# Three places in a hand-ordered mixer: a join after the activation sums, a forward set one channel pair earlier, token output's sums ahead of a forward set

## The chip, the cores and the metric

The kernel runs on one core of one Trainium2 chip. The metric is the device time of one execution in microseconds (us); lower is better. All data are float32. The abbreviations of the profile are used: PE is TensorE's matrix multiplication and PEld its weight load, DVE is VectorE, ACT is ScalarE, POOL is GpSimd and SP is the queue that issues most transfers.

## The reference

Eight sequences of 3008 tokens with 256 channels pass a global filter and then an MLP mixer.

```python
# x (8, 3008, 256), filt_r and filt_i (1505, 256)
X = np.fft.rfft(x, axis=1)
y = np.fft.irfft(X * (filt_r + 1j * filt_i), n=3008, axis=1)      # the filter
# w_tok1 (3008, 256), w_tok2 (256, 3008), w_ch1 (256, 1536), w_ch2 (1536, 256)
h = np.maximum(y.transpose(0, 2, 1) @ w_tok1, 0.0) @ w_tok2      # token mixing
u = y + h.transpose(0, 2, 1)
out = u + np.maximum(u @ w_ch1, 0.0) @ w_ch2                     # channel mixing
```

## The kernel before

**The mixer's items.** The program is one list of instructions for each engine, in an order that is written out by hand: each engine works off its own list and waits where a value or a buffer is not ready. The main loop, `mix`, goes over 288 items: 8 sequences b, 6 blocks of tokens m (512 wide, the last 448), and 6 channel pairs jp. An item works out two of the twelve 128-channel tiles of the hidden layer for one block. Both products of the channel mixing are done with seven half-size products in place of eight, which costs sums on DVE.

One item i issues, in this order:

- `up_first` (PE, L844): four products of u and of its sums v into the two PSUM tiles `ps_pg` (the two banks of that name, which every item uses); ACT copies one of them (L847).
- `up_middle` (DVE): the sum that the text calls u2, and a double sum s, both read `ps_pg`.
- one waiting step of `todo_v` (a list of small DVE steps), then `h_sums` (DVE) on item i-1's activated `hh`, which makes its four tiles t, and the first half of `down` (PE, L878) for item i-1. This is **place 0**.
- `up_last` (PE, L860): three more products into `ps_pg`; two DVE additions that leave the hidden values in `hh` (in the text: the hidden additions), each with its ReLU on ACT (L865); one more waiting step. This is **place 1**.
- the second half of `down` for item i-1 (four products with t). Where item i-1 was the last pair of its block, six steps of `finish` go into `todo_v`, and the first two, `a` and `b_`, are done at once: they read the four output banks `ps_po`, which the next item's `down` starts to fill anew. This is **place 2**.

All these DVE additions go through the helper `v` and stand in the profile as L822.

**The token mixing** for the next sequence lies inside this loop. At the third pair of a sequence's last block (item 32 of its 36) `token_sums` puts 48 products into one of the two PSUM banks `ps_acc` and `ps_b` (L721). At pairs 4 and 5 of that block `u_part` (L765) makes block 0 of the next u; `v_steps` then leaves two DVE steps in `todo_v`: the first makes two of the v tiles from u, the second (`t24`, two additions of 128x256) makes the other two. The next item, the first of the next sequence, reads all v in its `up_first`.

**The filter** of later sequences is another list of steps, `dft`, a generator which the main loop resumes at given places. Sequences are filtered in groups: (1, 2) beside the mixer of sequence 0; (3, 4) beside that of 1 and 2; (5, 6) beside 3 and 4; (7) beside 5 and 6. Each group ends with 16 pairs of frequencies, and a pair has three steps:

- "b", `b_pair`: the forward set, four small products (L501) into both `ps_acc` and `ps_b`, two DVE multiplications with the filter (L644) that read a bank each, and the issue of the loads for the pair two further on (SP);
- "m", `join`: two DVE operations on these products (L649, L650);
- "i", `bi_pair`: the inverse set, again four small products into the two banks, two ACT copies out of them (L630), and two stores (SP).

For the last three groups a table says at which (jp, place) the step that comes next is run, so a block of six items holds two frequency pairs:

```python
due = (jp, place) in {"b": ((5, 1), (2, 1)), "m": ((0, 0), (3, 0)), "i": ((1, 0), (3, 2))}[coming]
```

A generator step goes behind what its place names and ahead of what comes next. So the forward set at (5, 1) is joined at (0, 0) of the next block, between `h_sums` and `up_last`'s additions on DVE, and its inverse set follows at (1, 0). In the sequences 1, 3 and 5 these steps run on through the last block; in 2, 4 and 6 they are done before it, and in 7 there are none. The group (3, 4) or (5, 6) has twice the width of the group (7) in each of these operations.

Of the kernel before, what the change touches and what calls it, by code (L numbers as in the profile page):

```python
# [41 lines left out]
JP = JT // 2  # L42
# [3 lines left out]
MT = 6  # L46
# [73 lines left out]
def kernel(  # L120
# [591 lines left out]
    def t4_load(b, c, lo=PARTS[0], hi=P, queue=nc.sync):  # L712
        if lo == 0:
            t4[b, c] = t4p.tile([P, TC4, D], FP32, tag="t4", name="t4")
        queue.dma_start(t4[b, c][lo:hi], rows_of(g_d, b)[lo:hi, ts(c, TC4), :])
# [66 lines left out]
    def w2m_load(m):  # L782
        hw = width(m) // 2
        nc.sync.dma_start(w2m[m % 2][:, :, 0:hw], w2_d[m, :, :, 0:hw])
# [148 lines left out]
    def u_part(b, m, i):  # L933
        if i == 0:
            uts[b, m] = up.tile([P, DH, 512], FP32, tag="u", name="u")
        (u_quarter if b else u_unit)(b, m, h1s[b], uts[b, m], i)
# [13 lines left out]
    def one_step():  # L950
        if todo_v:
            todo_v.pop(0)()

    def mix(next_ready):

        wait = []
        pos, hhs, tts = {}, {}, {}

        def loads(b):
            if b + 1 < B and next_ready(b):  # L960
                for c in wait:
                    t4_load(b + 1, c)
                wait.clear()


        own = ({(4, 2): (0, 1)}, {(3, 0): (0,), (4, 0): (1,), (4, 2): (2, 3)})
        new = {(JP - 2, 0): (0, 1), (JP - 1, 0): (2, 3)}

        def u_parts(b, m, jp, place):
            parts = own[b > 0] if m + 1 < MT else new if b + 1 < B else {}  # L970
            now = parts.get((jp, place), ())
            b, m = (b, m + 1) if m + 1 < MT else (b + 1, 0)
            for part in now:
                u_part(b, m, part)
            if now and now[-1] == max(p for ps in parts.values() for p in ps):
                if m:
                    wait.append(m)
                todo_v.extend(v_steps(b, m))
                if b and (b, m) < (B - 1, MT - 2):
                    w2m_load((m + 2) % MT)  # L980

        to_dram = [f for m in range(MT) for f in w2_sums(m)]
        items = [(b, m, jp) for b in range(B) for m in range(MT) for jp in range(JP)]
        n = MT * JP
        for i in range(len(items) + 1):
            now, old = i < len(items), i >= 1
            if ended[0] < len(tiles):
                convert()
            if now:
                b, m, jp = items[i]  # L990
                if i % n == 0:
                    wait.append(0)
                w = width(m)
                hhs[i] = hp.tile([P, 4, 256], FP32, tag="hh", name="hh")
                g = [bank("pg").rearrange("p (s n) -> p s n", s=2) for _ in range(2)]
                s = up_first(jp, uts[b, m], vts[b, m], w, g)
                up_middle(hhs[i], w, g, s)
            one_step()
            if old:
                bo, mo, jo = items[i - 1]  # L1000
                tts[i - 1] = tp.tile([P, 4, 256], FP32, tag="t", name="t")
                for f in h_sums(hhs[i - 1], tts[i - 1], width(mo)):
                    f()
                down(mo, jo, 0, hhs[i - 1], tts[i - 1], pos.setdefault((bo, mo), []))
            if now:
                u_parts(b, m, jp, 0)
            yield b, i % n, 0
            if ended[0] < len(tiles):
                convert()
            if now:  # L1010
                up_last(jp, uts[b, m], vts[b, m], w, g, s, hhs[i])
            one_step()
            loads(b)
            yield b, i % n, 1
            if old:
                down(mo, jo, 1, hhs.pop(i - 1), tts.pop(i - 1), pos[bo, mo])
                if jo == JP - 1:
                    todo_v.extend(finish(bo, mo, uts[bo, mo], pos[bo, mo]))
                    one_step()
                    one_step()  # L1020
            if now:
                if b + 1 < B and i % n == n - 4:
                    h1s[b + 1] = token_relu(b + 1, token_sums(b + 1))
                u_parts(b, m, jp, 2)
                if jp == JP - 1:
                    while todo_v and m + 1 == MT:
                        one_step()
                if i >= 8 and to_dram:
                    to_dram.pop(0)()
                if i in (28, 29):  # L1030
                    w2m_load(i - 28)
            loads(b)
            yield b, i % n, 2
        while todo_v:
            one_step()

    with tc.manual_schedule():
        nc.sync.dma_start(wa0, wa0_d)
        nc.vector.memset(turned[:, A:K2, :], 0.0)
        for t in filts:  # L1040
            nc.vector.memset(t, 0.0)
        half = 0
        second = dft(GROUPS[1])
        for i, _ in enumerate(dft(GROUPS[0])):
            if i == 0:
                nc.scalar.dma_start(wai_t, wait_d)
            k = i - NXC - 2

            if i < NXC:
                if i in (1, 3, 5, 7, 9):  # L1050
                    start()
                if i == NXC - 1:
                    copies()
                    for t, src in ((wa, wa_d), (was, was_d), (wai, wai_d), (ident, ident_d)):
                        nc.scalar.dma_start(t, src)
            elif k >= 0:
                if k == K2 - 5:
                    pause.append(True)
                while half < 2 * IN_B * (k + 1) // K2:
                    if half % 2:  # L1060
                        convert_end()
                    else:
                        convert_middle()
                    half += 1

                if 19 <= k < 25:
                    t4_load(0, k - 19, 0, PARTS[1])
                elif 26 <= k < 29:
                    for c in range(2):
                        t4_load(0, 2 * (k - 26) + c, PARTS[1], PARTS[2])  # L1070
                elif k in (30, 31):
                    for c in range(3):
                        t4_load(0, 3 * (k - 30) + c, PARTS[2], PARTS[3])
        pause.clear()

        fill(5)
        for c in range(A // TC4):
            t4_load(0, c, PARTS[3], P, (nc.sync, nc.gpsimd)[c % 2])
        both = wcp.tile([P, 2, JP, 7, P], FP32, tag="wc", name="wc")

        chan.extend((both[:, 0], both[:, 1]))
        next(second)
        for i in range(IN_B, A // 2 + TC * W2G):
            convert()
            if i == A // 2 + BY_PE - 1:
                sum_up()
                acc = token_sums(0)

        ahead[0](XF, nc.gpsimd)
        h1s[0] = token_relu(0, acc)  # L1090
        for dh in range(DH):
            convert()
            u_part(0, 0, dh)
        for f in v_steps(0, 0):
            f()
        for _ in range(XB):
            next(second)
        group, todo, done = -1, iter(()), True

        def next_ready(b):  # L1100
            return done or b != GROUPS[group][-1]

        coming = "a"
        for b, i, place in mix(next_ready):
            if group + 1 < len(GROUPS) and b == GROUPS[group + 1][0]:
                if not done:
                    raise AssertionError("the filter's steps don't fit beside the mixer's")
                group += 1  # L1110
                done = group + 1 == len(GROUPS)
                todo = iter(()) if done else dft(GROUPS[group + 1]) if group else second
                coming = "a"
            if done:
                continue
            jp = i % JP
            if coming in "aw":
                due = place == 1 or group == 0
            elif group:
                due = (jp, place) in {"b": ((5, 1), (2, 1)), "m": ((0, 0), (3, 0)), "i": ((1, 0), (3, 2))}[coming]  # L1120
            else:
                due = (jp - (coming == "i")) % JP in ((5, 1, 2, 3) if i < 4 * JP else (5, 0, 1, 2, 3)) and place == {"b": 1, "m": 2, "i": 0}[coming]
            if due:
                coming = next(todo, "end")
                done = coming == "end"
# [30 lines left out]
```

## Time and profile before

| | |
|---|---|
| time, median of 3 runs | 2497.85 us (2496.29 to 2501.91) |
| profiled execution, its time | 2499.35 us |
| profiled execution, its span of instructions | 2497.6 us |
| mean granted TensorE clock | 0.993 |
| busy in the span: PE, PEld, DVE, ACT, POOL | 97%, 79%, 74%, 27%, 24% |
| PE busy from 300 to 2300 us | 98.5% to 99.7% in each stretch of the seven looked at |

The time of the profiled execution is 1.75 us more than its span. Shares are of the span from the first to the last instruction. A row of a timeline gives the start, the length, the engine, the line, the operation with what it writes and reads, how many instructions are merged, and in brackets the idle time of the engine ahead of it with what ended it. A row of the waits gives the total in us, how often, and the longest one. A 128x256 product stands as two matmul records.

### The profile page before, as it was taken

The numbers are of one execution on the slowest core, as the hardware profiler recorded it, in microseconds if no ns is written. First come the engines' busy times: TensorE is split into PE (matmuls) and PEld (weight loads), VectorE is DVE, ScalarE is ACT, GpSimd is POOL, SyncE is SP. The second block draws the span as 40 slices with busy tenths as digits, with TensorE's granted clock in tenths as the row PEclk, the third lists the DMA queues.
The fourth block names the chain that finished last, engine by engine and source line by source line (L and its number), as shares of the span: only waits on it lengthen the run. The fifth ranks groups of instructions, "written<-read, shape, count | busy, mean of one in ns | idle before, by whom it ended". The sixth has DMA issues, their size and how long they took to land.

```text
span 2497.6 us, 33945 instructions
## 1 busy us (share of the span) xinstructions
PE 2420.1 (97%) x11836; PEld 1962.4 (79%) x11836; DVE 1846.7 (74%) x3404; ACT 678.6 (27%) x1348; POOL 598.4 (24%) x1086
## 2 busy tenths in 40 slices
PE   7888999999999999999999999999999999999997
PEld 3556676877788777887778877897888888898887
DVE  7686878587885878667885788758786678757776
ACT  5633222133221222223221222213221222212221
POOL 6473332212111211211121112111212112212121
PEclk9999999999999999999999999999999999999999
DMA  9973444254321222335332323314322121301100
GB/s 217 252 206 118 123 131 144 76 170 131 109 82 53 82 82 61 94 99 172 89 94 62 86 71 83 103 45 126 86 77 72 49 70 43 98 24 29 39 16 18
DMA packets 173122, 236.07 MB, mean 95 GB/s; under 512 B 33213, under 2 KB 123067, under 8 KB 172952
## 3 DMA queue, kind: packets, MB, share of 16 engines
q1 hardware_dynamic: 128344, 175.53, 24.1%
q0 software_dynamic: 33376, 48.46, 7.8%
q10 hardware_dynamic: 11232, 9.92, 1.3%
q8 instruction: 94, 1.54, 0.3%
q14 instruction: 76, 0.62, 0.1%
HBM read 156.56 MB, written 77.22 MB: 94 GB/s over the span
## 4 chain that ended last, share of the span: by engine, by line
PE 44%; DVE 5%; issue 1%; DMA 0%; ACT 0%; DVEq 0%; POOL 0%; SPq 0%; ACTq 0%; POOLq 0%
PE ps_po L878 17%; PE ps_pg L844 10%; PE ps_pg L860 7%; PE ps_b L721 2%; PE ps_acc L721 2%; PE ps_b L765 2%; PE ps_acc L765 2%; DVE t L822 1%; DVE hh L822 1%; PE ps_acc L501 1%; DVE p L644 1%; PE ps_b L501 1%; PE ps_b L743 1%; PE ps_acc L743 1%; DVE s L822 1%
## 5 line engine op out<-in xcount | busy, mean ns | idle before, releaser
L925 POOL DMA_DIRECT2D out_dram<-r x757 | 412.5, 553 | 1672.4 <-ACT hh L865 1408.4
L822 DVE TENSOR_TENSOR hh<-ps_pg,s 128x512 f32<-128x512 f32 (+3 forms) x864 | 482.6, 586 | 390.2 <-ACT s L847 386.8
L865 ACT ACTIVATE hh<-hh 128x512 f32<-128x512 f32 (+1 forms) x576 | 348.3, 623 | 986.2 <-DVE hh L822 986.2
L878 PE MATMUL ps_po<-t,wc 128*128 128x256 f32 (+1 forms) x2304 | 546.6, 380 | 4.2 <-DVE t L822 3.1
L878 PEld LDWEIGHTS ps_po<-t,wc 128*128 128x128 f32 x2304 | 426.3, 190 | 132.4 <-DVE t L822 41.1
L844 PE MATMUL ps_pg<-v,wc 128*128 128x256 f32 (+1 forms) x1728 | 415.5, 377 | 2.1 <-DVE v L822 2.1
L878 PE MATMUL ps_po<-hh,wc 128*128 128x256 f32 (+1 forms) x1728 | 413.5, 375 | 0.2 <-ACT hh L865 0.2
L844 PEld LDWEIGHTS ps_pg<-v,wc 128*128 128x128 f32 x1728 | 327.8, 191 | 43.5 <-DVE v L822 5.9
L878 PEld LDWEIGHTS ps_po<-hh,wc 128*128 128x128 f32 x1728 | 329.1, 191 | 38.2 <-ACT hh L865 0.5
L860 PE MATMUL ps_pg<-u,wc 128*128 128x256 f32 (+1 forms) x1152 | 295.8, 379 | 6.0 <-DVE hh L822 6.0
L860 PEld LDWEIGHTS ps_pg<-u,wc 128*128 128x128 f32 x1152 | 215.5, 190 | 63.7 <-DVE hh L822 30.5
L822 DVE TENSOR_TENSOR t<-t,hh 128x256 f32<-128x256 f32 (+1 forms) x576 | 245.2, 426 | 19.9
L822 DVE TENSOR_TENSOR s<-ps_pg,hh 128x512 f32<-128x512 f32 (+1 forms) x288 | 196.1, 681 | 30.3 <-DVE hh L822 0.5
L822 DVE TENSOR_TENSOR t<-hh 128x512 f32<-128x512 f32 (+1 forms) x288 | 192.9, 670 | 0.6 <-ACT hh L865 0.6
L847 ACT COPY s<-ps_pg 128x256 f32<-128x256 f32 (+1 forms) x288 | 106.2, 369 | 318.4 <-PE ps_pg L844 316.9
L844 PE MATMUL ps_pg<-u,wc 128*128 128x256 f32 (+1 forms) x576 | 173.8, 383 | 14.0 <-DVE hh L822 14.0
L860 PE MATMUL ps_pg<-v,wc 128*128 128x256 f32 (+1 forms) x576 | 168.8, 375 | 0.0
L844 PEld LDWEIGHTS ps_pg<-u,wc 128*128 128x128 f32 x576 | 105.6, 190 | 51.6 <-DVE hh L822 37.0
L860 PEld LDWEIGHTS ps_pg<-v,wc 128*128 128x128 f32 x576 | 109.3, 190 | 12.6
L822 DVE TENSOR_TENSOR u<-ps_b,u 128x256 f32<-128x256 f32 (+2 forms) x102 | 58.3, 572 | 67.5 <-PE ps_b L765 61.8
L822 DVE TENSOR_TENSOR u<-ps_acc,u 128x512 f32<-128x512 f32 (+2 forms) x108 | 62.4, 577 | 56.5 <-PE ps_acc L765 52.2
L721 PE MATMUL ps_b<-t,w 128*128 128x256 f32 x384 | 83.9, 380 | 8.1 <-DVE p L644 4.7
(140 smaller groups left out, 2464.7 us busy)
## 6 DMA issues: line engine op xcount, KB each, us to landing
w<-w_tmp SPq DMA_DIRECT2D x35, 896.0 KB
out_dram<-r POOLq DMA_DIRECT2D x698, 32.0 KB, 2.7
t<-g_tmp SPq DMA_DIRECT2D x42, 512.0 KB
g_tmp<-t SPq DMA_DIRECT2D x96, 192.0 KB
t<-z_tmp SPq DMA_DIRECT2D x180, 96.0 KB
z_tmp<-t SPq DMA_DIRECT2D x60, 256.0 KB
filt<-in_x_dram SPq DMA_DIRECT2D x90, 128.0 KB
wb<-wbi_t SPq DMA_DIRECT2D x64, 128.0 KB
```

The lines of the kernel that those rows point to most:

```text
L501: nc.tensor.matmul(outs(i, j), stat(i, j), mov(i, j), start=True, stop=True)
L644: nc.vector.tensor_tensor(out=prods[c, h], in0=pss[h].unsqueeze(1).to_broadcast([P, 2, nb, D]), in1=filts[c % FB][:, :, 0, :].unsqueeze(2) ...
L721: nc.tensor.matmul(acc[:, t, :], w1[:, a, ts(t, P)], t4[b, a // TC4][:, a % TC4, :], start=(a == 0 and t == 0), stop=(a == A - 1 and t == ...
L743: nc.tensor.matmul(ps[:, ds(q * P, n)], t4[b, c][:, r, ts(dh, P)], wai[:, 0:n], start=(first and q == 0), stop=(not first and q == 3))
L765: nc.tensor.matmul(ps[:, ds(j * hw, hw)], h1[:, n, :], w2m[m % 2][:, at, 0:hw], start=(i < 2 and j == 0), stop=(j == len(todo) - 1))
L822: nc.vector.tensor_tensor(out=out, in0=in0, in1=in1, op=op)
L844: nc.tensor.matmul(ps[:, 0:hw], chan[0][:, jp, n, :], mov, start=True, stop=True)
L847: nc.scalar.copy(out=s[:, 0], in_=g[0][:, 0, 0:hw])
L860: nc.tensor.matmul(ps[:, 0:hw], chan[0][:, jp, n, :], mov, start=True, stop=True)
L865: nc.scalar.activation(out=hs, in_=hs, func=AF.Relu)
L878: nc.tensor.matmul(po[i][:, j, 0:hw], chan[1][:, jp, n, :], mov, start=(jp == 0 and first == 1), stop=(jp == JP - 1 and last == 1))
L925: q.dma_start(bass.AP(tensor=ob.tensor, offset=ob.offset + row * D + g * cw, ap=[[N1 * D, 32], [D if h else -D, n], [1, cw]]), blocks[ts(g ...
```

## The change

Four lines are altered. After place 1's own waiting step, the last item of every sequence does one more step of `todo_v`; that step is `t24`. In the table, the forward set that was at (2, 1) is run at (1, 1) where the block is the sequence's last, and the join that was at (0, 0) is run at (0, 1). `n` is the number of items of a sequence, 36.

```diff
             one_step()
+            if now and i % n == n - 1:
+                one_step()
             loads(b)
             yield b, i % n, 1
...
         coming = "a"
+        n = MT * JP
         for b, i, place in mix(next_ready):
...
-                due = (jp, place) in {"b": ((5, 1), (2, 1)), "m": ((0, 0), (3, 0)), "i": ((1, 0), (3, 2))}[coming]
+                due = (jp, place) in {"b": ((5, 1), (1 if i >= n - JP else 2, 1)), "m": ((0, 1), (3, 0)), "i": ((1, 0), (3, 2))}[coming]
```

No operation is added or taken away. Sequence 0 takes another line for its due places, which is not changed, and none of its steps come after item 31.

## The prediction

> **What bounds the kernel.** The page's first part comes first: TensorE is busy for nearly the whole span, and everything else is far below it.
>
> ```profile
> PE 2420.1 (97%) x11836; PEld 1962.4 (79%) x11836; DVE 1846.7 (74%) x3404; ACT 678.6 (27%) x1348; POOL 598.4 (24%) x1086
> ```
>
> So only what makes PE stand still can be won or lost. The change touches sequences 1 to 6, hence the waits of PE in two windows: 600 to 1780 us (groups of two sequences) and 1780 to 2250 us (the group of one).
>
> ```profile
> PE ps_pg L844 <- DVE hh L822: 4.7, 16, 0.6
> PE ps_b L721 <- DVE p L644: 3.6, 2, 1.8
> PE ps_pg L844 <- DVE v L822: 1.8, 2, 0.9
> PE ps_po L878 <- DVE t L822: 1.2, 4, 0.4
> ...
> PE ps_b L721 <- DVE p L644: 1.1, 1, 1.1
> PE ps_po L878 <- DVE t L822: 0.8, 2, 0.4
> PE ps_pg L844 <- DVE v L822: 0.3, 1, 0.3
> ```
>
> Every wait of PE there is for DVE. The first row counts 16, as many as there are joins at (0, 0) in these two groups (8 each), and in the timeline each stands behind such a join. One of them, at sequence 2, block 3:
>
> ```profile
> 943.54 1.89 PE L878 MATMUL ps_po<-t,wc 128*128 128x256 f32 x8
> 943.72 0.69 DVE L649 TENSOR_TENSOR p<-p,p 128x512 f32<-128x512 f32 x1
> 944.32 0.69 DVE L650 TENSOR_TENSOR p<-p,p 128x512 f32<-128x512 f32 x1
> 944.92 1.28 DVE L822 TENSOR_TENSOR hh<-ps_pg,s 128x512 f32<-128x512 f32 x2
> 945.64 0.63 ACT L865 ACTIVATE hh<-hh 128x512 f32<-128x512 f32 x1 [4.92 <-DVE hh L822]
> 945.66 0.30 PEld L844 LDWEIGHTS ps_pg<-u,wc 128*128 128x128 f32 x2 [0.63 <-DVE hh L822]
> 945.66 0.70 PE L844 MATMUL ps_pg<-u,wc 128*128 128x256 f32 x2 [0.23 <-DVE hh L822]
> ```
>
> The join holds DVE from 943.72 to 944.92; only then do the hidden additions empty `ps_pg`, which the next item's `up_first` is to fill. Eight matmuls in 1.89 us with 0.38 us each start 0.216 us apart, so a bar reaches 0.16 us into the next: a stall costs PE the idle time shown and 0.16 us more, here 0.40.
>
> The last two places, the token sums (754.50, for a bank) and the first item of sequence 2 (800.04, for v):
>
> ```profile
> 753.24 1.21 DVE L644 TENSOR_TENSOR p<-ps_b,filt 128x1024 f32<-128x1024 f32 x1
> 754.50 0.70 PE L721 MATMUL ps_b<-t,w 128*128 128x256 f32 x2 [1.79 <-DVE p L644]
> ...
> 798.44 1.22 DVE L644 TENSOR_TENSOR p<-ps_acc,filt 128x1024 f32<-128x1024 f32 x1
> 799.57 0.88 DVE L822 TENSOR_TENSOR v<-v,u 128x256 f32<-128x256 f32 x2
> 800.04 1.13 PE L844 MATMUL ps_pg<-v,wc 128*128 128x256 f32 x4 [0.91 <-DVE v L822]
> ```
>
> **What the Trainium skill says.** "Perfetto Trace Analysis", section Identifying the Most-Contended Engine, holds busy matmul time for a bad measure of headroom, since matmuls overlap; section Optimization Strategy has one look for the gaps and what ends them. The trace agrees: the 0.16 us are such an overlap. The same page, section Per-engine timelines, lets a DVE instruction signal only once its writes are acknowledged, the end of its bar. Here the first hidden addition ends at 945.60 (944.92 and 0.68) and PE starts at 945.66: 0.06 us for a hand-over. "VectorE: DVE Perf Modes", section The TRN2 errata, gives (N + 151)/0.96 ns for a float32 two-tensor add: 691 ns for 512 elements, 1224 for 1024. The trace has 0.68 to 0.71 and 1.21 us. I use the trace's.
>
> **Part 1, the join behind the hidden additions (24 joins).** In the 16 wide ones two operations, 1.20 us from start to start, go behind 1.28 us of additions. `up_last` is through at 943.70 (its last row 943.11 and 0.59), `h_sums` at 943.81: the additions can start where the join did, and end near 945.0. `up_first` then follows `down` without a gap. DVE does the same work in the same order of sums, so `a`, the first step of `finish`, stays at 946.12 and the wait for `ps_po` doesn't grow. DVE even gains: its second step there waited 0.36 us for an ACT copy (L890) that stood behind the ReLUs, and these come 1.2 us earlier. So what follows on DVE moves forward by some 0.4 us together with PE. The join is needed at (1, 0), from 948.88; it ends at 946.2.
> Twelve of the 16 stand alone: 4.7 less 0.31 (two, part 2) and 0.67 (two, part 3) is 3.7, and 12 x 0.16 is 1.9: 5.6 us. The two largest (0.57 and 0.65 shown) exceed what DVE can follow; I take off 0.4. **Gain 5.2 us**, between 0 (DVE holds PE up one item later instead) and 5.6. The 8 narrow joins (0.42 us an operation) show no wait of PE: nothing, as both orders are hidden behind `down`; 0.3 us either way.
>
> **Part 2, t24 ahead of the last forward set (ends of sequences 1, 3, 5).** Two additions, 0.88 us, go ahead of two multiplications, 2.4 us. Shown: 0.91, 0.90 and 0.27, with 0.16 each 2.6 us. Where no set lies between (sequences 0, 2, 4, 6) the same place still loses 0.15 us; that stays. Gain 2.1. The multiplications end 0.9 us later, near 800.5, and u2 behind them started at 801.23 after 0.79 us of idle waiting for ACT: it can start at 800.5, so nothing is late. Two of these items have a join stall of part 1 too (0.15 and 0.16 shown), 0.6 us, which goes as well. **Gain 2.7 us**, 1.5 to 3. In the four other sequences no DVE operation lies between the two places: nothing.
>
> **Part 3, the forward set one channel pair ahead of the token sums (3 sets).** It moves all it issues: four products (1.02 us of PE, 0.7 narrow), two multiplications (2.4 us of DVE, 1.3 narrow), 13 issues on SP. SP: the loads are for the pair two further on, over 40 us away; they go ahead of nothing due before that. PE: the set needs the banks that the inverse set of (1, 0) left; ACT's copies out of them end at 744.04, by then 0.5 us earlier, and the set's turn is at 743.6: just in time, at most 0.2 us a set.
> What goes, with 0.16 each: at the token sums 1.79, 1.79 and 1.15 (5.2 us); one item before, waits of `down` for t of 0.17, 0.17 and 0.33 (1.2 us), covered by the set's own products now; the join stall of these blocks, 2 x 0.5 us. Together 7.4 us.
> What comes: at jp 2 the multiplications stand ahead of u2, s, a transpose (0.70), `h_sums`. Counted through on DVE: the multiplications run from 746.45 to 748.85, u2 to 749.24 (`up_last` needs it, and was due at 748.98), s to 749.97, transpose to 750.6, the first of `h_sums` to 751.1. `down` starts at 751.2, the token sums 1.5 us behind it at 752.7 in place of 754.50: 1.8 us twice. The narrow one in the same way: 1920.1 in place of 1921.65, 1.55. **Gain 5.1 us**; a new wait of about 0.8 us for each wide set at jp 2 is what is late next. Bounds 1.5 (the new wait takes the old one's place) and 7.4.
>
> **Sum.** 5.2 + 2.7 + 5.1 = 13.0 us. The profiled execution's span is 2497.6, its time 2499.35: they would be 2484.6 and 2486.3. The median, 2497.85, lies 1.5 us below that execution; from it, **2484.8 us**. A measurement of this kernel can tell about 0.2%, 5.0 us, from no change.
>
> **Rivals.**
> *DVE stays the bound.* It is busy without a gap from the forward set at (5, 1) to jp 1. If it doesn't give up the 0.36 us, the stall of part 1 comes back at jp 1 as a wait for t. For: without a filter step, `down` at pair 1 of the last block already waits 0.44 us for t. Against: the wide joins' next item has none. Then part 1 gives 0, parts 2 and 3 some 5: 2493. Chance 0.14.
> *The early forward set only shifts the wait*, to u2 and t at jp 2, and keeps the banks' copies in PE's way. Part 3 then gives 1.5: 2488.5. Chance 0.14.
> *Slower: the join delays `finish`.* If the hidden additions can't start before the join would have been over anyway, `a` slips by the join's 1.29 us. The next `down` fills `ps_po` at 947.50, and `a`'s first step left it at 946.80: slack of 0.7. With 0.6 us lost 16 times, the old stalls kept (0.4 each), and narrow joins losing 0.4, part 1 costs 13 us against 8 gained: 2503. It decides when `up_last` ends more than 0.7 us behind `h_sums`; here it ends 0.1 before. Chance 0.04.
> The likeliest case keeps 0.68.
>
> **How the numbers follow.** All that is shown gone, and nothing in its place, is 5.6 + 2.7 + 7.4 + 0.3 = 16.0 us: 2481.9; with 2 us for the median, 2480. At the other end the range takes in the first rival: 2493.5. The likeliest case and the second rival are faster by over 0.2%; the first rival lies on the bound, and I give it mostly to no change. Faster 0.84, within 0.2% 0.12, slower 0.04.
>
> **What would show it.** Right: PE's waits at L844 for hh gone (16 to 0 or a few) in 600 to 1780 us; L649 behind the hidden additions; the L890 wait of DVE smaller than 17.7 us; the token sums' wait gone, with a wait of under 1 us for t or u2 before them; the wait for v gone. Wrong: more and longer waits at L878 for t (first rival), waits there of about 1 us in the token sums' items (second), waits at L878 for `ps_po` after each join (third).

## The result, and the profile after

The changed kernel takes 2481.34 us (median of 4 runs, 2479.32 to 2483.14) against 2497.39 us (4 runs, 2496.29 to 2501.91): a ratio of 0.9934 with a 95% interval of 0.9922 to 0.9947. That is faster by 0.66%, some 16 us, where 13.0 us were forecast. The profiled execution took 2483.14 us with a span of 2481.4, which is 16.2 us shorter than the span before.

The busy line of the page hardly moves: the same work is done, with less standing still.

```profile
PE 2417.7 (97%) x11836; PEld 1965.7 (79%) x11836; DVE 1845.1 (74%) x3404; ACT 679.7 (27%) x1348; POOL 598.4 (24%) x1086
```

The waits of PE in the two windows of before, 600 to 1780 us and 1780 to 2250 us (total, times, longest; the three dots part the windows):

```profile
PE ps_po L878 <- DVE t L822: 1.7, 4, 0.4
PE ps_po L878 <- DVE u L822: 0.2, 1, 0.2
...
PE ps_po L878 <- DVE t L822: 0.4, 1, 0.4
```

The 16 waits for the hidden additions (L844 for hh), the three of the token sums (L721) and the three for v are gone. What is new is small: a wait of `down` for `finish`'s first sum (u), and, within the row for t, a wait at pair 2 of the two blocks with a wide early set (0.42 us each), where two smaller ones at pair 1 (0.17 each) have gone.

The timeline at sequence 2, block 3, the join that the prediction showed:

```profile
938.60 1.89 PE L878 MATMUL ps_po<-t,wc 128*128 128x256 f32 x8
938.77 1.28 DVE L822 TENSOR_TENSOR hh<-ps_pg,s 128x512 f32<-128x512 f32 x2
939.49 1.23 ACT L865 ACTIVATE hh<-hh 128x512 f32<-128x512 f32 x2 [3.71 <-DVE hh L822]
939.97 0.68 DVE L649 TENSOR_TENSOR p<-p,p 128x512 f32<-128x512 f32 x1
940.11 0.41 PEld L844 LDWEIGHTS ps_pg<-u,wc 128*128 128x128 f32 x2
940.33 0.59 PE L844 MATMUL ps_pg<-u,wc 128*128 128x256 f32 x2
...
940.62 0.36 ACT L890 COPY r<-ps_po 128x256 f32<-128x256 f32 x1
...
941.17 0.69 DVE L822 TENSOR_TENSOR u<-ps_po,u 128x512 f32<-128x512 f32 x1
...
941.77 0.42 DVE L822 TENSOR_TENSOR r<-ps_po,r 128x256 f32<-128x256 f32 x1
```

The hidden additions start 0.17 us behind `down`'s first matmul, where they started 1.38 us behind it. `up_first` (940.33) follows the eight matmuls of `down` in step: 8 x 0.216 behind 938.60. ACT's copy L890 is done at 940.98, before DVE asks for it at 941.77, so the bracket of 0.36 us that this row had is gone as well. In before, the first two sums of `finish` stood like this:

```profile
946.12 0.68 DVE L822 TENSOR_TENSOR u<-ps_po,u 128x512 f32<-128x512 f32 x1
...
947.17 0.42 DVE L822 TENSOR_TENSOR r<-ps_po,r 128x256 f32<-128x256 f32 x1 [0.36 <-ACT r L890]
```

The second sum started 1.05 us behind the first; now it is 0.60.

The token sums of sequence 1's end, and the first item of sequence 2:

```profile
746.75 1.22 DVE L644 TENSOR_TENSOR p<-ps_b,filt 128x1024 f32<-128x1024 f32 x1
...
750.17 1.78 PE L878 MATMUL ps_po<-t,wc 128*128 128x224 f32 x8 [0.42 <-DVE t L822]
...
751.79 3.40 PE L721 MATMUL ps_b<-t,w 128*128 128x256 f32 x15
```

```profile
794.60 0.88 DVE L822 TENSOR_TENSOR v<-v,u 128x256 f32<-128x256 f32 x2
795.46 1.23 DVE L644 TENSOR_TENSOR p<-ps_b,filt 128x1024 f32<-128x1024 f32 x1
...
796.15 1.46 PE L844 MATMUL ps_pg<-v,wc 128*128 128x256 f32 x6
```

The multiplications end at 747.97, long before the token sums, which start without a bracket; in their place `down`, just ahead of them, waits 0.42 us for t. In the second view the v sums stand ahead of the multiplications, and `up_first` runs through.

**A measure finer than the median.** ACT's copy L847 comes once in every item, so the same items can be compared between two timelines. From the copy of sequence 1's first item to that of sequence 7's last, before takes 501.61 to 2477.17, 1975.56 us; after takes 1959.16. This leaves out the start, where that first copy comes anywhere between 496.2 and 503.6 us in the nine profiles of this study. Inside the stretch the granted clock is 1.00 in all nine, and sequence 7 has no filter step and takes 234.15 to 234.18 us in before, after and the first four experiments, so hundredths count. The gain in this stretch, item by item:

| step | forecast | measured |
|---|---|---|
| 12 wide joins that stand alone | 5.2 | 5.5 (0.45 each) |
| 7 narrow joins that stand alone | 0 | 1.8 (0.21 to 0.32 each) |
| t24, with the join behind it in two places | 2.7 | 3.0 (1.22, 1.22, 0.53) |
| forward set, with the join of its block | 5.1 | 6.2 (2.10, 2.10, 1.97) |
| sum (of unrounded figures) | 13.0 | 16.4 |

### The profile page after: what moved, and what is told of

It is laid out like the page before. It is cut to its first block, busy times and chain, and to the rows that moved or that the text cites. A ratio compares the mean times of both kernels' runs of the same rounds, so it can differ in the third digit from the quotient of the medians.

```text
span 2481.4 us, 33945 instructions
## 1 busy us (share of the span) xinstructions
PE 2417.7 (97%) x11836; PEld 1965.7 (79%) x11836; DVE 1845.1 (74%) x3404; ACT 679.7 (27%) x1348; POOL 598.4 (24%) x1086
## 4 chain that ended last, share of the span: by engine, by line
PE 48%; DVE 2%; DMA 0%; issue 0%; ACT 0%; POOL 0%; SPq 0%; DVEq 0%; POOLq 0%; ACTq 0%
PE ps_po L878 19%; PE ps_pg L844 11%; PE ps_pg L860 8%; PE ps_acc L721 2%; PE ps_b L721 2%; PE ps_b L765 2%; PE ps_acc L765 2%; PE ps_b L501 1%; PE ps_acc L501 1%; PE ps_acc L743 1%; PE ps_b L743 1%; DVE t L822 1%; DVE hh L822 0%; DVE u L822 0%; DVE s L822 0%
## 5 line engine op out<-in xcount | busy, mean ns | idle before, releaser
L844 PE MATMUL ps_pg<-v,wc 128*128 128x256 f32 (+1 forms) x1728 | 415.8, 377 | 0.1
L844 PEld LDWEIGHTS ps_pg<-v,wc 128*128 128x128 f32 x1728 | 328.5, 191 | 40.9 <-DVE v L822 2.6
L860 PE MATMUL ps_pg<-u,wc 128*128 128x256 f32 (+1 forms) x1152 | 295.2, 379 | 5.7 <-DVE hh L822 5.7
L860 PEld LDWEIGHTS ps_pg<-u,wc 128*128 128x128 f32 x1152 | 214.9, 190 | 62.6 <-DVE hh L822 31.4
L847 ACT COPY s<-ps_pg 128x256 f32<-128x256 f32 (+1 forms) x288 | 106.0, 368 | 333.7 <-PE ps_pg L844 332.4
L844 PE MATMUL ps_pg<-u,wc 128*128 128x256 f32 (+1 forms) x576 | 172.4, 381 | 9.3 <-DVE hh L822 9.3
L860 PE MATMUL ps_pg<-v,wc 128*128 128x256 f32 (+1 forms) x576 | 168.7, 375 | 0.0
L844 PEld LDWEIGHTS ps_pg<-u,wc 128*128 128x128 f32 x576 | 107.2, 190 | 41.5 <-DVE hh L822 26.0
L860 PEld LDWEIGHTS ps_pg<-v,wc 128*128 128x128 f32 x576 | 109.2, 190 | 12.6
L721 PE MATMUL ps_acc<-t,w 128*128 128x256 f32 x384 | 83.5, 379 | 0.0
```

The source lines that it names most:

```text
L721: nc.tensor.matmul(acc[:, t, :], w1[:, a, ts(t, P)], t4[b, a // TC4][:, a % TC4, :], start=(a == 0 and t == 0), stop=(a == A - 1 and t == ...
L844: nc.tensor.matmul(ps[:, 0:hw], chan[0][:, jp, n, :], mov, start=True, stop=True)
L847: nc.scalar.copy(out=s[:, 0], in_=g[0][:, 0, 0:hw])
L860: nc.tensor.matmul(ps[:, 0:hw], chan[0][:, jp, n, :], mov, start=True, stop=True)
```

## The experiments

"Stretch" below is the one just defined, against the 1975.56 us of before unless another kernel is named.

### Each part alone

The join alone:

```diff
-"m": ((0, 0), (3, 0))
+"m": ((0, 1), (3, 0))
```

> The kernel before with the join alone moved from place 0 to place 1. Theory (the three parts stand alone, and a stall costs TensorE its shown idle, the 0.16 us of overlap and about 0.1 us of restart): 16 wide joins give 0.45 us each and 8 narrow ones 0.25 each, 9.2 us in all, and DVE's wait for the ACT copy L890 falls from 17.7 to about 9 us. Rival (a gained stall is partly given back where the token sums or the v tiles still make TensorE wait): only the 12 wide joins that stand alone count, 5.5 us.

Measured: 2488.05 us, ratio 0.9957 (0.9944 to 0.9971); the stretch is 9.4 us shorter, and DVE's wait for L890 is 9.0 us. The waits of PE from 600 to 2250 us:

```profile
PE ps_b L721 <- DVE p L644: 4.7, 3, 1.8
PE ps_pg L844 <- DVE v L822: 2.1, 3, 0.9
PE ps_po L878 <- DVE t L822: 1.3, 3, 0.4
PE ps_po L878 <- DVE u L822: 0.2, 1, 0.2
```

The hh row has gone, and the row for t has fallen from 2.0 us in six waits to 1.3 in three; the token sums and the v sums wait as long as before. The four wide joins next to them gain 0.40 to 0.42 us each as well: nothing is given back there, and the rival's 5.5 us are out.

The forward set alone:

```diff
-"b": ((5, 1), (2, 1))
+"b": ((5, 1), (1 if i >= n - JP else 2, 1))
```

> The kernel before with the forward set alone moved one channel pair ahead of the token sums. Theory (parts stand alone): 2.1 us at each of the two wide places less the 0.45 us that the join there is worth, and 1.7 us at the narrow one: 5.0 us; the token sums wait for nothing, and down waits for t at pair 2 by about 0.4 us shown. Rival (the set can come earlier only because the join has left DVE free): about 3 us.

Measured: 2492.92 us, ratio 0.9978 (0.9968 to 0.9987); the stretch is 5.3 us shorter (1.70 twice at the wide places, 1.70 at the narrow one). The waits of PE from 600 to 1780 us:

```profile
PE ps_pg L844 <- DVE hh L822: 4.6, 16, 0.6
PE ps_pg L844 <- DVE v L822: 1.8, 2, 0.9
PE ps_po L878 <- DVE t L822: 1.8, 4, 0.5
```

The L721 row is gone, and `down` waits for t by up to 0.5 us. The set doesn't need the join out of its way.

t24 alone:

```diff
             one_step()
+            if now and i % n == n - 1:
+                one_step()
             loads(b)
```

> The kernel before with t24 alone moved ahead of the last forward set. Theory (parts stand alone): 0.95 us at two places and 0.4 at the third, 2.3 us; the wait at L844 for v disappears, the 16 waits at L844 for hh stay. Rival (u2 comes late behind the later multiplications): under 1 us, and a wait at L860 for hh in the first item of sequences 2, 4 and 6.

Measured: 2495.70 us, ratio 0.9990 (0.9982 to 0.9999); the stretch is 2.1 us shorter. The two wide places gain 1.17 us each and lose 0.48 again one item later, 0.69 net; the narrow one gains 0.53. The waits of PE from 600 to 1780 us:

```profile
PE ps_pg L844 <- DVE hh L822: 5.6, 16, 0.6
PE ps_b L721 <- DVE p L644: 3.6, 2, 1.8
PE ps_po L878 <- DVE t L822: 1.2, 4, 0.4
```

The v row is gone, but the hh row has grown from 4.7 to 5.6 us: PE comes earlier to the join's stall of the next item and waits longer there. With the join moved too, this stall is gone and the place is worth 1.22 us. No wait at L860 shows, so the rival is out.

The three gains sum to 9.4 + 5.3 + 2.1 = 16.8 us; together they give 16.4. The parts stand alone, to within 0.4 us.

### The join one place later still

```diff
-"m": ((0, 0), (3, 0))
+"m": ((0, 2), (3, 0))
```

> The kernel before with the join alone moved to place 2, behind the finish sums a and b_ as well. Theory (the join must also fill the time in which DVE waits for down's second half and the ACT copy): DVE stands idle ahead of a, the join ends near the inverse set's turn, u2 comes no earlier than before, and the inverse set waits for L650 by up to 0.5 us; the 16 waits at L844 for hh go, but the time changes by 0 to 2 us either way. Rival (only the early release of ps_pg counts): as much as the join at place 1, 9 us faster.

Measured: 2497.03 us, ratio 0.9994 (0.9985 to 1.0002); the stretch is 0.4 us shorter. Each wide join gains the same 0.54 to 1.06 us at its own item as at place 1, and gives it back, whole or nearly so (0.44 to 1.05), at the next. The timeline at the same block:

```profile
943.09 0.42 DVE L822 TENSOR_TENSOR r<-ps_po,r 128x256 f32<-128x256 f32 x1 [0.36 <-ACT r L890]
...
944.69 0.68 DVE L649 TENSOR_TENSOR p<-p,p 128x512 f32<-128x512 f32 x1
945.29 0.69 DVE L650 TENSOR_TENSOR p<-p,p 128x512 f32<-128x512 f32 x1
...
945.53 1.15 PE L501 MATMUL ps_b<-p,wb 64*64 64x512 f32 x3
945.89 0.42 DVE L822 TENSOR_TENSOR hh<-ps_pg,s 128x256 f32<-128x256 f32 x1
...
947.69 0.68 DVE L822 TENSOR_TENSOR t<-hh 128x512 f32<-128x512 f32 x1
```

DVE meets ACT's copy too early and stands idle for 0.36 us. The join ends at 945.98, after the inverse set's start at 945.53: `up_last` begins 1.51 us behind that start, against 1.02 in before. Nor does t come earlier: counted from this block's `down` at pair 0, it starts after 7.01 us (947.69 less 940.68), in before after 7.02 and in the changed kernel after 6.55. The late inverse set is therefore not what takes the gain back; `down` would have to wait for t in any case. So freeing `ps_pg` early moves the stall by one item, no more. What keeps the gain at place 1 is that the join lies where DVE would otherwise wait for the copy. One detail of the expectation was wrong: `a` itself began at once; only its second sum waited.

### Why the narrow joins gained

The changed kernel wins 0.25 us at each narrow join, where no wait of PE was shown. Two causes were possible: hidden additions that come 0.7 us earlier, or DVE's 0.36 us wait for L890. The second can be taken away without moving a join, by another order of `finish`'s sums in the kernel before:

```diff
         def a():
             v(us[:, 0], p23, us[:, 0])
-            v(u2, p16[:, 1], p1)
+            v(us[:, 1], p45, us[:, 1])
 
         def b_():
-            v(us[:, 1], p45, us[:, 1])
+            v(u2, p16[:, 1], p1)
```

> The kernel before with finish's sums in another order: the second big sum goes ahead of the one that reads the ACT copy L890; join, set and t24 stay as before. Theory (DVE's 0.36 us wait for L890 is what makes t late at pair 1, in the narrow blocks and in those with no filter step): DVE's wait for L890 falls from 17.7 to under 4 us, the narrow blocks lose their 0.25 us each (2 us) and the blocks with no filter step some 0.25 us each where they now wait (about 4 us): 4 to 6 us faster; the 16 waits at L844 for hh stay. Rival (the narrow blocks gained because the hidden additions came earlier): no change.

Measured: 2487.18 us, ratio 0.9967 (0.9955 to 0.9980); the stretch is 8.0 us shorter, and no wait for L890 is left. The narrow blocks gain 0.22 to 0.32 us each (0.41 in the last block of sequence 5), to 0.02 us the same, block by block, as with the join alone moved. So the copy is the cause, and the rival is out. The narrow block at sequence 5, block 3, in before and then in this kernel:

```profile
1820.45 0.42 DVE L822 TENSOR_TENSOR r<-ps_po,r 128x256 f32<-128x256 f32 x1 [0.36 <-ACT r L890]
...
1823.85 0.69 DVE L822 TENSOR_TENSOR t<-hh 128x512 f32<-128x512 f32 x1
...
1824.08 0.59 PE L860 MATMUL ps_pg<-v,wc 128*128 128x256 f32 x2
...
1824.68 1.97 PE L878 MATMUL ps_po<-t,wc 128*128 128x256 f32 x8
```

```profile
1811.84 0.41 DVE L822 TENSOR_TENSOR r<-ps_po,r 128x256 f32<-128x256 f32 x1
...
1814.63 0.68 DVE L822 TENSOR_TENSOR t<-hh 128x512 f32<-128x512 f32 x1
...
1815.32 0.59 PE L860 MATMUL ps_pg<-v,wc 128*128 128x256 f32 x2
...
1815.75 1.89 PE L878 MATMUL ps_po<-t,wc 128*128 128x256 f32 x8
```

In before, t ends at 1824.54 and `down` starts 0.60 us behind the last row of `up_last`; here it is 0.43, which is in step. The eight matmuls take 1.97 us there and 1.89 here. The two differences, 0.17 and 0.08, are the 0.25 us, though no bracket stands at `down` in before: the modelled bar of the matmul ahead of it covers the wait. That it is a wait for t shows in another distance. `down` starts 0.14 us behind the end of t, as it does at the seven places from 600 us on where before has a bracket for t.

The gain was larger than the 4 to 6 us expected, because the wide blocks gained too: 0.17 us in twelve of them and 0.40 in two. In before, `down` at pair 1 starts the same 0.14 to 0.15 us behind the end of t in these fourteen. With the sums in the other order it follows `up_last` in step.

### Versions beyond the change

What is left after the change is mostly `down` waiting for t at pairs 1 and 2, where a step of `finish` stands ahead of `h_sums`. On top of the changed kernel:

```diff
-            one_step()
+            behind_sums = now and jp in (1, 2)
+            if not behind_sums:
+                one_step()
             if old:
...
                     f()
+                if behind_sums:
+                    one_step()
                 down(mo, jo, 0, hhs[i - 1], tts[i - 1], pos.setdefault((bo, mo), []))
```

> The changed kernel, and at pairs 1 and 2 of each block the waiting finish step (two sums, or the first transpose) goes behind h_sums in place of ahead of it. Theory (what is left of TensorE's waits in sequences 0 to 7 is for t, which these steps hold up): the 16 waits at L878 for t go, 0.3 to 0.7 us each with the restart, 8 us faster than the changed kernel, near 2473. Rival (the steps only move, and hold up the hidden additions or the transposes instead): within 2 us of the changed kernel.

Measured: 2471.75 us, ratio to before 0.9905 (0.9890 to 0.9920); the stretch is 7.0 us shorter than the changed kernel's. From 600 to 2250 us:

```profile
PE ps_pg L844 <- DVE hh L822: 0.6, 3, 0.2
PE ps_po L878 <- DVE u L822: 0.2, 1, 0.2
```

Of the t waits none is left; some 0.2 us stalls for the hidden additions are what the rival named, far too small to matter.

> The changed kernel with both: the waiting step behind h_sums at pairs 1 and 2, and finish's sums in the other order. Theory: the order of finish's sums gives nothing more where the steps are already out of the way, and makes ps_po's third bank come free 0.7 us later: the same as with the steps alone, or up to 2 us slower, with waits at L878 for the sum that reads p16. Rival (they add up): 2 to 4 us faster than with the steps alone.

Both edits on the changed kernel: 2468.45 us, ratio to before 0.9889 (0.9876 to 0.9903), an interval that does not touch the changed kernel's. This is the lowest median of the study, though its interval overlaps that of the steps alone. The stretch is 8.1 us shorter than the changed kernel's, 1.1 more than with the steps alone: my theory, nothing more or a loss, was wrong, and 1.1 is less than the 2 to 4 of the rival. The feared wait for `ps_po` is a single one of 0.2 us, the same as without the new order; the extra gain comes in the blocks with no filter step, 0.06 to 0.13 us each, where the L890 wait was still there. From 600 to 2250 us one row is left:

```profile
PE ps_po L878 <- DVE u L822: 0.2, 1, 0.2
```

## Why the prediction was right, and where it was short

The direction and the likeliest case held, and its mechanism in the main; the time, 2481.3, lies 3.5 us under the 2484.8 forecast and inside the range.

- **Part 1, wide joins.** The cause was right, but that the sum came out (5.5 for 5.2) was in part luck. The forecast priced each stall by its bracket; the twelve joins gained 0.44 to 0.46 us each, whether the bracket was 0.22 or 0.65. That is what DVE gained between its first two sums of `finish`: 1.05 less 0.60 us. In all twelve blocks, `down` of pair 1 starts 0.15 us behind the end of t both in before and in the changed kernel, so PE follows DVE there, in waits too short for a bracket. The prediction held it against its first rival that the wide joins' next item has no wait for t; it has one. The step "DVE even gains" by the L890 wait was the one that mattered: without it (the join at place 2) the gain is nothing.
- **Part 1, narrow joins: the step that failed.** "Nothing, as both orders are hidden behind `down`" was read from the wait row, which shows no stall. They gained 1.8 us, since the L890 wait made t late there too; 0.27 us of what the narrow forward set gained (1.97, against 1.70 with the set alone) goes with the join of its block as well. The prediction had the 0.36 us in hand for the wide joins and didn't carry it to the narrow ones.
- **Part 2.** 3.0 for 2.7. That nothing would be late behind the multiplications held: u2 starts at 797.74, right behind them.
- **Part 3.** The mis-sized term was the new wait at pair 2, put at about 0.8 us; its bracket is 0.42, or 0.58 with the overlap. The DVE count gave 751.2 for `down`'s start and 752.7 for the token sums on before's clock. The items ahead had moved by 0.71 us when this block began, so the measured 750.17 and 751.79 stand for 750.9 and 752.5. Also left out, here and in part 2, was the slow restart of PE described below, about 0.1 us a stall. This part gave 6.2 for 5.1. ACT's copies out of the banks were indeed just in time: the set starts at 743.16, 0.15 us after the later of them ends (743.01).
- **The rivals.** "DVE stays the bound" would have been right for a join at place 2; at place 1 DVE still sets the pace of the wide blocks, but gives up its 0.36 us. "Only shifts the wait" has its 0.42 us and no more. "The join delays `finish`" shows in small: four of the wide blocks wait 0.13 to 0.20 us (0.30 to 0.37 with the overlap) for `finish`'s first sum, where the old stall went whole.

## What to carry to other kernels

At the wide joins, taking away a stall of PE paid only where DVE, which feeds it, also got faster in the same stretch. Look for such idle time of the feeding engine (here DVE's 0.36 us for an ACT copy) and put the moved work there; one place further on, the same move was worth nothing. And compare start times of matmuls between alike items: a start that comes 0.17 us late leaves no bracket, yet such starts at the narrow joins made up nearly 2 of the 16 us.

## What was not expected of the hardware

After a stall PE restarts slowly here. Two matmuls of L844 right behind the stall took 0.70 us in before (945.66), and 0.59 in the changed kernel (940.33): the second starts 0.11 us late. At all 16 stalls of this row it is 0.10 to 0.11. Before the stalled row the weight load had no lead (it starts at 945.66 too); in step it leads by 0.2 us. So a stall costs its bracket, 0.16 us of overlap and about 0.1 us of restart, which is 0.50 us for the bracket of 0.23. The slow second start goes with the missing lead, and not with standing still as such: in before, from 600 to 2250 us, the mixer's first matmul behind the filter's small products (L501) has a weight load without a lead too. It has no idle time ahead of it, and still the second matmul starts 0.32 us behind it (104 places of full width), where 0.22 is in step. That the one causes the other is an inference; no run tested it by itself.
